# Relu sums of the sixth up product put first for all four row tiles, low parts of that quarter on GpSimd

## The chip, the cores and the metric

The kernel runs on one core of one Trainium2 chip. The metric is the device time of one execution in microseconds (us). Engines are named as in the profile: PE is the matrix engine (PEld its weight loads), DVE is VectorE, ACT is ScalarE, POOL is GpSimd, SP issues most DMAs. Each works through its own instructions in the order in which they are written; between engines an instruction waits for semaphores.

## The reference, cut to what matters

The program is a linear attention followed by two mixture layers. The change lies in the first of them, whose eight experts all run on all 2304 tokens:

```python
for e in range(E):                      # E = 8
    h = np.maximum(x @ w1[e], 0.0)      # x: 2304 x 512, w1[e]: 512 x 1024
    ye = h @ w2[e]                      # w2[e]: 1024 x 512
    out += P[:, e:e + 1] * ye
```

## The kernel before

The 2304 tokens are worked on in three blocks of 768 and each block by eight experts, so the loop over s runs 24 times; one pass is a step. Steps 8 to 22 are "fast" steps: both their products are done in seven half-size block products instead of eight (a Winograd form of Strassen's scheme), at the price of sums and differences before and after. Every float32 operand of a product is split into a high part and a low part, and a product is three matmuls: high by high, high by low, low by high.

The up products of a step (`fill`, L968) are numbered n = 0 to 6. Each has four row tiles i, and each tile is six matmuls of 384 columns into one PSUM bank. Products 1, 4 and 6 add to the banks of products 0, 3 and 5. Product 6 is the one that the change calls the sixth. Behind each tile, DVE and ACT turn the bank into the hidden layer's quarters, `hq["11"]`, `hq["12"]`, `hq["22"]` and `hq["21"]`, each with a high part [0] and a low part [1].

For tile i of product 6, with p the tile's bank, DVE adds `qs` to p in place (L1279), adds relu(p) to the buffer `s2b`, called d (L1280), writes relu(p) + u3 into `qs`, called q (L1283), and writes relu(p) - r11 into `r11`, called r (L1284). ACT rounds d into the high part `hq["21"][0]` (L1282). `run_pend()` (L1281) lets DVE do one difference left over from product 5 (L1273), only behind tile 0. Behind the last tile, DVE makes the four low parts `hq["21"][1]` from d and its high part (L1296).

Then `down` runs seven down products m = 0 to 6 of three row groups j, each 12 matmuls of 256 columns (L1104), 36 in a product. Their left operands are, in order, the quarters 11, 12, 21, and then 11, 12, 22, 21, where 11, 12 and 21 are filled anew: from `r11` by ACT at L1149 and by DVE at L1150, from `qs` by ACT at L1152 and by POOL at L1154, from `r12` by ACT at L1156 and by POOL at L1158. During product m = 0, POOL subtracts d from `r12` in four pieces (L1163). Behind products 0 and 2, ACT copies the PSUM result aside (L1123); behind product 1, DVE adds to it (L1125) and to the accumulators (L1117). For products 5 and 6 of the up stage and elsewhere, POOL makes low parts: L1274 for the quarter 22, L166 for weights. Low parts of products 1 and 4 are DVE's (L953).

PSUM: all these tiles come from one ring of six banks, `psA`, handed out in order. Each fast step takes sixteen in the up stage (four each at n = 0, 2, 3 and 5) and six in the down stage: two at m = 0 (for j = 0 and j = 2), two at m = 1, two at m = 4. So counting on from the four banks of products 5 and 6, m = 0 takes the two banks that remain, m = 1 takes the banks of tiles 0 (for j = 0) and 1 (for j = 2), and m = 4 those of tiles 2 and 3. A matmul that begins a bank waits until the last reader of its earlier tile is done.

Of the kernel before, what the change touches and what calls it, by code (L numbers as in the profile page):

```python
# [13 lines left out]
ALU = mybir.AluOpType  # L14
# [26 lines left out]
def f32(ap):  # L41
    return ap.bitcast(F32)

@with_exitstack
def tile_linattn_moe_moe(ctx: ExitStack, tc: tile.TileContext, qT, k, v, g2, wg, w1a, w2a, emb, embT, tau, w1b, w2b, out):
    nc = tc.nc
# [22 lines left out]
    def ps_a():  # L69
        return get(psA, [P, 512], F32, "A", 6)  # L70
# [61 lines left out]
    r11, r12, s2b, s5 = (rawbig[:, i * 4 * HB:(i + 1) * 4 * HB].rearrange("p (k n) -> p k n", k=4) for i in range(4))  # L132
# [430 lines left out]
    u3 = up.tile([P, 4, HB], F32, name="u3")  # L563
    rb = up.tile([P, 2, D], F32, name="rb")
    xrow = qs.rearrange("p k n -> p (k n)")
    hq = {}
# [74 lines left out]
    def run_hooks(n=1):  # L641
        for _ in range(n):
            if hooks:
                hooks.pop(0)()
# [292 lines left out]
    def open_late():  # L937
        hp4 = late.enter_context(tc.tile_pool(name="h4", bufs=1, side="right", reuse_waits="tile"))
        open_h(hp4, ("12", "22"))
        accp = late.enter_context(tc.tile_pool(name="acc", bufs=1, side="right", reuse_waits="tile"))  # L940
        accs[0] = [accp.tile([P, D], F32, name=f"acc{t}") for t in range(JT)]
# [5 lines left out]
    def run_pend():  # L947
        while pend:
            pend.pop(0)()

    def low(a, i, src):
        hh, hl = hq[a]
        nc.vector.scalar_tensor_tensor(hl[:, i, :], src, 0.0, f32(hh[:, i, :]), ALU.max, ALU.subtract)  # L953

    def hidden(a, i, ps, u, dst):
        nc.vector.tensor_tensor(dst, ps, u, ALU.add)  # L956
        run_pend()
        nc.scalar.activation(hq[a][0][:, i, :], dst, AF.Relu)  # L958
        pend.append(lambda: low(a, i, dst))

    def fill(ps, g, i, n, first, last):
        wh, wl = parts[g]
        xh, xl = x_part(n, 0), x_part(n, 1)
        j = 0
        for kk in range(2):
            fs = slice(kk * 512 + i * P, kk * 512 + (i + 1) * P)
            for a, bb in ((wh, xh), (wh, xl), (wl, xh)):
                nc.tensor.matmul(  # L968
                    ps[:, 0:HB], a[:, fs], bb[:, kk, :], start=(first and j == 0), stop=(j == 5), skip_group_check=True)
                j += 1  # L970
# [3 lines left out]
    def ahead(g):  # L974
        h = g + 3
        if h < len(seq_of):
            s, n = seq_of[h]
            if s < E or h in plain_at or n >= 7 and not quick(s):
                pool = n in POOL_LOW and (s, n) != (NSTEP - 1, 9) if s < E or not quick(s) and n >= 7 else True
                prep(h, nc.gpsimd if pool else None)  # L980
            else:
                fetch(h)
            keep(h - 1)
        for h in plain_load.get(g, ()):
            load_plain(h)
        s, n = seq_of[g]
        loads = []
        if (s < E or s == NSTEP - 1) and n < 3:
            loads = [lambda q=q: load_second(s, q) for q in (W2ORDER[0:2], W2ORDER[2:3], W2ORDER[3:4])[n]]
        if s + 1 < E and n in (3, 4, 7):  # L990
            loads = [lambda w=w: load_quarter(s + 1, w) for w in {3: ("w11", "w21"), 4: ("w22",), 7: ("w12",)}[n]]
        elif s + 1 < E and n in (5, 6):
            spare(s + 1, "s1" if n == 5 else "s2")
        for f in loads:
            if after_two:
                after_two.append([2, f])
            else:
                f()
        if s == NSTEP - 1 and n > 2:
            for f in {3: [lambda: early_w1(0), lambda: early_w1(1)], 4: [lambda: early_w1(2)], 5: [lambda: early_w1(3)],  # L1000
                      6: [lambda: early_w2(0)], 7: [lambda: early_w2(1)]}.get(n, ()):
                f()
# [35 lines left out]
    def run_thooks():  # L1038
        run_after()
        if s >= 2:  # L1040
            for f in thooks.pop(tick[0], ()):
                f()
            tick[0] += 1
# [152 lines left out]
    n_hooks = len(hooks)  # L1196
    dhooks = []
    xq = []

    for s in range(NBK * E):  # L1200
        blk, e = divmod(s, E)
# [36 lines left out]
        for n in range(7):  # L1238
            g = base[s] + n
            if s == 0 and n == 4:  # L1240
                assert len(hooks) <= n_hooks - n_att
                atts.close()
                open_late()
            for i in range(4):
                if n in (0, 2, 3, 5):
                    bank[n, i] = ps_a()
                ps = bank[{1: 0, 4: 3, 6: 5}.get(n, n), i]
                fill(ps, g, i, n, n in (0, 2, 3, 5), n in (1, 4, 6))
                p = ps[:, 0:HB]
                if n == 0:  # L1250
                    nc.scalar.copy(qs[:, i, :], p)  # L1251
                elif n == 1:
                    nc.scalar.activation(hq["11"][0][:, i, :], p, AF.Relu)
                    if fast:
                        nc.scalar.activation(r11[:, i, :], p, AF.Relu)  # L1255
                    low("11", i, p)
                elif n == 2:
                    nc.vector.tensor_tensor(qs[:, i, :], p, qs[:, i, :], ALU.add)
                elif n == 3:
                    nc.vector.tensor_tensor(u3[:, i, :], p, qs[:, i, :], ALU.add)  # L1260
                elif n == 4:
                    hidden("12", i, p, qs[:, i, :], p)
                    if fast:
                        nc.scalar.activation(r12[:, i, :], p, AF.Relu)
                elif n == 5 and not fast:
                    hidden("22", i, p, u3[:, i, :], u3[:, i, :])
                elif n == 5:
                    u = u3[:, i, :]
                    nc.vector.tensor_tensor(u, p, u, ALU.add)
                    run_pend()  # L1270
                    nc.scalar.activation(u, u, AF.Relu)
                    nc.scalar.copy(hq["22"][0][:, i, :], u)
                    pend.append(lambda i=i, u=u: nc.vector.tensor_tensor(s2b[:, i, :], u, r11[:, i, :], ALU.subtract))  # L1273
                    nc.gpsimd.tensor_tensor(hq["22"][1][:, i, :], u, f32(hq["22"][0][:, i, :]), ALU.subtract)  # L1274
                elif not fast:
                    hidden("21", i, p, qs[:, i, :], p)
                else:
                    d, r, q = s2b[:, i, :], r11[:, i, :], qs[:, i, :]
                    nc.vector.tensor_tensor(p, p, q, ALU.add)  # L1279
                    nc.vector.scalar_tensor_tensor(d, p, 0.0, d, ALU.max, ALU.add)  # L1280
                    run_pend()  # L1281
                    nc.scalar.copy(hq["21"][0][:, i, :], d)  # L1282
                    nc.vector.scalar_tensor_tensor(q, p, 0.0, u3[:, i, :], ALU.max, ALU.add)  # L1283
                    nc.vector.scalar_tensor_tensor(r, p, 0.0, r, ALU.max, ALU.subtract)  # L1284
                if i == 1:
                    ahead(g)
                if n > 0 and i == 2 and squared:
                    squared.pop(0)()
                run_hooks()
                if fast and n < 4 and dhooks:  # L1290
                    dhooks.pop(0)()
                run_thooks()
        run_pend()
        if fast:
            for i in range(4):
                nc.vector.tensor_tensor(hq["21"][1][:, i, :], s2b[:, i, :], f32(hq["21"][0][:, i, :]), ALU.subtract)  # L1296
        if e == E - 1 and blk + 1 < NBK and not fast:
            xq = x_steps(*x_stage(blk + 1))
        if e == 2 and blk == 0:
# [500 lines left out]
```

## Time and profile before

| what | us |
|---|---|
| median of 3 runs (lowest, highest) | 1817.12 (1816.57, 1821.68) |
| the profiled execution | 1814.65 |
| its span from first to last instruction | 1812.9 |
| PE busy | 1782.2 |
| DVE busy | 1253.0 |
| POOL busy | 995.5 |
| ACT busy | 845.3 |

The profiled execution's own time is 1.75 us more than its span, and 2.47 us below the median of the runs. In a timeline a row is one instruction or several like ones merged: start, time from first start to last end, engine, line, operation, what is written and read, count. A row's instructions may overlap, since the engines are pipelined.

### The profile page before, as it was taken

Reading aid. Unit: us, or ns where it says so; the run is one execution under the profiler, and the core shown is the slowest. Engines: PE = TensorE matmul, PEld = TensorE weight load, DVE = VectorE, ACT = ScalarE, POOL = GpSimd, SP = SyncE. Lnnn points to the kernel's source line nnn. Section 1 sums busy time; section 2 is a strip of 40 time slices with the busy share of each in tenths; the row PEclk is TensorE's granted clock in tenths of the full one; section 3 lists DMA queues with packets and bytes.
Section 4 is the critical chain, followed back from the end, with each engine's and each line's share of the span. In section 5 each row is a group of like instructions: output and inputs, shape, how many; then the busy total and the mean of one; then the engine's idle time right before and its main releaser. Section 6 shows DMA issues by size and latency. Waiting matters only on the chain. (4 is left out here: it accounts for less than half of the span.)

```text
span 1812.9 us, 30972 instructions
## 1 busy us (share of the span) xinstructions
PE 1782.2 (98%) x11494; PEld 1689.0 (93%) x11494; DVE 1253.0 (69%) x2196; ACT 845.3 (47%) x1435; POOL 995.5 (55%) x813
## 2 busy tenths in 40 slices
PE   7999999999999999999999999999999999999997
PEld 7889889989988999999999999999999998888996
DVE  3755596566647789876556779997567763877665
ACT  3645344344434643554444553454454433556443
POOL 1422378889879555664456475655466332543222
PEclk8999999999999999999999999999999999999999
DMA  9626267779768856556465666566465653588664
GB/s 303 219 67 210 94 226 281 252 285 333 270 244 280 285 203 222 194 190 220 166 223 193 244 224 235 188 214 215 169 213 183 229 201 109 185 315 276 231 231 154
DMA packets 185568, 397.73 MB, mean 219 GB/s; under 512 B 16448, under 2 KB 86592, under 8 KB 185408
## 3 DMA queue, kind: packets, MB, share of 16 engines
q1 hardware_dynamic: 179680, 378.33, 60.1%
q0 software_dynamic: 4000, 13.11, 2.1%
q10 hardware_dynamic: 1728, 4.23, 0.7%
q8 instruction: 92, 1.51, 0.3%
q14 instruction: 68, 0.56, 0.1%
HBM read 314.61 MB, written 81.00 MB: 218 GB/s over the span
## 5 line engine op out<-in xcount | busy, mean ns | idle before, releaser
L968 PE MATMUL A<-xo,wh 128*128 128x384 f32 x2688 | 687.8, 337 | 1.9 <-ACT qs L1251 1.4
L968 PEld LDWEIGHTS A<-xo,wh 128*128 128x128 f32 x2688 | 482.5, 188 | 4.3 <-ACT qs L1251 2.1
L968 PE MATMUL A<-xo,wl 128*128 128x384 f32 x1344 | 452.1, 336 | 1.4 <-POOL wl L166 1.4
L1104 PE MATMUL A<-wh,d 128*128 128x256 f32 x2520 | 441.4, 279 | 0.8 <-POOL d L1158 0.6
L166 POOL TENSOR_TENSOR wl<-raw,wh 128x512 fp32r<-128x512 f32 x180 | 248.9, 1405 | 284.0 <-ACT wh L161 117.4
L1104 PEld LDWEIGHTS A<-wh,d 128*128 128x128 f32 x2520 | 382.7, 188 | 4.2 <-POOL d L1158 0.8
L1104 PE MATMUL A<-wl,d 128*128 128x256 f32 x1260 | 348.7, 277 | 0.0
L968 PEld LDWEIGHTS A<-xo,wl 128*128 128x128 f32 x1344 | 252.6, 188 | 2.6 <-POOL wl L166 2.6
L1317 PE MATMUL A<-wh,d 128*128 128x512 f32 x768 | 243.8, 392 | 0.0
L1104 PEld LDWEIGHTS A<-wl,d 128*128 128x128 f32 x1260 | 236.6, 188 | 0.0
L953 DVE SCALAR_TENSOR_TENSOR d<-A,d 128x384 fp32r<-128x384 f32 x228 | 126.0, 553 | 158.1 <-ACT raw L1255 87.9
L166 POOL TENSOR_TENSOR wl<-rb,wh 128x512 fp32r<-128x512 f32 x92 | 127.5, 1407 | 161.2 <-ACT wh L161 161.2
L1317 PEld LDWEIGHTS A<-wh,d 128*128 128x128 f32 x768 | 144.2, 188 | 29.8 <-issue 0.3
L958 ACT ACTIVATE d<-A 128x384 fp32r<-128x384 f32 x132 | 65.6, 498 | 197.2 <-DVE A L956 194.9
L1317 PE MATMUL A<-wl,d 128*128 128x512 f32 x384 | 149.5, 389 | 0.0
L1251 ACT COPY qs<-A 128x384 f32<-128x384 f32 x96 | 45.7, 480 | 186.3 <-PE A L968 181.8
L161 ACT CAST wh<-raw 128x1024 fp32r<-128x1024 f32 x94 | 98.4, 1047 | 12.6 <-DMA raw<-in_w1a_dram 3.6
L260 DVE TENSOR_TENSOR wl<-raw,wh 128x1024 fp32r<-128x1024 f32 x45 | 70.8, 1575 | 35.6 <-ACT wh L259 30.3
L1317 PEld LDWEIGHTS A<-wl,d 128*128 128x128 f32 x384 | 72.2, 188 | 14.0
L956 DVE TENSOR_TENSOR A<-A,qs 128x384 f32<-128x384 f32 x132 | 73.6, 560 | 16.7 <-PE A L968 16.4
L1154 POOL TENSOR_TENSOR d<-qs,d 128x384 fp32r<-128x384 f32 x60 | 55.6, 958 | 45.5 <-ACT d L1152 45.5
L1260 DVE TENSOR_TENSOR u<-A,qs 128x384 f32<-128x384 f32 x96 | 52.1, 553 | 31.4 <-PE A L968 31.2
(496 smaller groups left out, 3365.4 us busy)
## 6 DMA issues: line engine op xcount, KB each, us to landing
raw<-in_w1a_dram SPq DMA_DIRECT2D x64, 512.0 KB, 4.4
wh<-w1c SPq DMA_DIRECT2D x64, 512.0 KB, 4.6
wl<-w1c SPq DMA_DIRECT2D x64, 512.0 KB, 5.9
wh<-w2c SPq DMA_DIRECT2D x60, 512.0 KB, 5.2
wl<-w2c SPq DMA_DIRECT2D x60, 512.0 KB, 6.0
raw<-in_w2a_dram SPq DMA_DIRECT2D x51, 512.0 KB, 4.3
raw<-in_w1b_dram SPq DMA_DIRECT2D x48, 512.0 KB, 5.4
raw<-in_w2b_dram SPq DMA_DIRECT2D x48, 512.0 KB, 4.3
```

The source lines that it names most:

```text
L161: nc.scalar.copy(hi, raw)
L166: eng.tensor_tensor(lo[:, c], raw[:, c], f32(hi[:, c]), ALU.subtract)
L260: after_two.append([2, lambda: nc.vector.tensor_tensor(lo, src, f32(hi), ALU.subtract)])
L953: nc.vector.scalar_tensor_tensor(hl[:, i, :], src, 0.0, f32(hh[:, i, :]), ALU.max, ALU.subtract)
L956: nc.vector.tensor_tensor(dst, ps, u, ALU.add)
L958: nc.scalar.activation(hq[a][0][:, i, :], dst, AF.Relu)
L968: nc.tensor.matmul(ps[:, 0:HB], a[:, fs], bb[:, kk, :], start=(first and j == 0), stop=(j == 5), skip_group_check=True)
L1104: nc.tensor.matmul(o, a[:, f, ts_], bb[:, ds_], start=(m in first and j != 1 and i == 0), stop=(i == 11), skip_group_check=True)
L1154: nc.gpsimd.tensor_tensor(a12[1][:, i], qs[:, i], f32(a12[0][:, i]), ALU.subtract)
L1251: nc.scalar.copy(qs[:, i, :], p)
L1260: nc.vector.tensor_tensor(u3[:, i, :], p, qs[:, i, :], ALU.add)
L1317: nc.tensor.matmul(ys[j], a, bb[:, ds_], start=(m + ff + i == 0), stop=(m == 3 and ff == 1 and i == 2))
```

## The change

The last two DVE operations of each tile of product 6 (q and r) are no longer issued in the tile's turn. They are kept in a list and issued behind the fourth tile, in the order q0, r0, q1, r1, q2, r2, q3, r3. The four low parts of the quarter 21 are issued to POOL instead of DVE. Nothing else is edited; the order of the matmuls and of the DMA issues stays.

```diff
                     nc.vector.scalar_tensor_tensor(d, p, 0.0, d, ALU.max, ALU.add)
                     run_pend()
                     nc.scalar.copy(hq["21"][0][:, i, :], d)
-                    nc.vector.scalar_tensor_tensor(q, p, 0.0, u3[:, i, :], ALU.max, ALU.add)
-                    nc.vector.scalar_tensor_tensor(r, p, 0.0, r, ALU.max, ALU.subtract)
+                    tails.append(lambda p=p, q=q, r=r, u=u3[:, i, :]: (
+                        nc.vector.scalar_tensor_tensor(q, p, 0.0, u, ALU.max, ALU.add),
+                        nc.vector.scalar_tensor_tensor(r, p, 0.0, r, ALU.max, ALU.subtract)))
...
         run_pend()
+        while tails:
+            tails.pop(0)()
         if fast:
             for i in range(4):
-                nc.vector.tensor_tensor(hq["21"][1][:, i, :], s2b[:, i, :], f32(hq["21"][0][:, i, :]), ALU.subtract)
+                nc.gpsimd.tensor_tensor(hq["21"][1][:, i, :], s2b[:, i, :], f32(hq["21"][0][:, i, :]), ALU.subtract)
```

## Rows read from the trace of the kernel before

**Rows 1.** Part 1 of the page: busy us, share of span, instructions.

```profile
PE 1782.2 (98%) x11494; PEld 1689.0 (93%) x11494; DVE 1253.0 (69%) x2196; ACT 845.3 (47%) x1435; POOL 995.5 (55%) x813
```

**Rows 2.** Line 1279 alone: count, ns min/median/max, first and last start.

```profile
L1279 DVE TENSOR_TENSOR A<-A,qs x60: 550/554/556, 617.5 to 1443.1; 128x384 f32<-128x384 f32 x60
```

**Rows 3.** Waits of PE from 600 to 1470: us in total, times, longest.

```profile
PE A L1104 <- POOL d L1158: 0.6, 1, 0.6
PE A L1104 <- ACT u L1123: 0.2, 1, 0.2
```

**Rows 4.** Down products 0 to 3, one step: length, busy per engine, PEclk, DMA, GB/s.

```profile
967.83:971.94 4.11, 4.11 (x37) 4.11 (x37) 4.04 (x10) 1.03 (x2) 4.11 (x5) 1.00 0.88 318
971.94:976.02 4.08, 4.08 (x38) 4.08 (x37) 4.05 (x9) 2.08 (x5) 2.05 (x3) 1.00 0.88 330
976.02:980.43 4.41, 4.41 (x39) 4.32 (x37) 4.38 (x7) 3.05 (x3) 1.87 (x2) 1.00 0.81 288
980.43:984.58 4.15, 4.15 (x39) 4.15 (x38) 0.93 (x3) 3.18 (x4) 3.98 (x5) 1.00 0.12 48
```

**Rows 5.** Timeline of PE in product 2 of that step: start, us, what.

```profile
976.59 0.39 PE L1104 MATMUL A<-wh,d 128*128 128x256 f32 x2
...
976.93 0.50 PE L1104 MATMUL A<-wh,d 128*128 128x256 f32 x2
...
977.40 0.50 PE L1104 MATMUL A<-wh,d 128*128 128x256 f32 x2
```

**Rows 6.** Timeline of DVE around the same step's up end at 967.83.

```profile
965.42 1.45 DVE L1273 TENSOR_TENSOR raw<-u,raw 128x384 f32<-128x384 f32 x1 [0.49 <-ACT u L1271]
966.79 0.55 DVE L1279 TENSOR_TENSOR A<-A,qs 128x384 f32<-128x384 f32 x1
967.38 0.56 DVE L1280 SCALAR_TENSOR_TENSOR raw<-A,raw 128x384 f32<-128x384 f32 x1
967.86 0.58 DVE L1273 TENSOR_TENSOR raw<-u,raw 128x384 f32<-128x384 f32 x1
968.36 0.55 DVE L1283 SCALAR_TENSOR_TENSOR qs<-A,u 128x384 f32<-128x384 f32 x1
968.83 0.54 DVE L1284 SCALAR_TENSOR_TENSOR raw<-A,raw 128x384 f32<-128x384 f32 x1
...
974.80 0.55 DVE L1284 SCALAR_TENSOR_TENSOR raw<-A,raw 128x384 f32<-128x384 f32 x1
975.27 2.08 DVE L1296 TENSOR_TENSOR d<-raw,d 128x384 fp32r<-128x384 f32 x4
977.27 1.75 DVE L1150 TENSOR_TENSOR d<-raw,d 128x1536 fp32r<-128x1536 f32 x1
978.93 0.69 DVE L1125 TENSOR_TENSOR A<-A,u 128x512 f32<-128x512 f32 x1
```

**Rows 7.** Timeline of ACT in the same step.

```profile
975.62 1.49 ACT L1149 CAST d<-raw 128x1536 fp32r<-128x1536 f32 x1
...
979.73 0.59 ACT L1123 COPY u<-A 128x512 f32<-128x512 f32 x1 [1.25 <-DVE A L1125]
```

**Rows 8.** Timeline of POOL in the same step.

```profile
965.16 2.87 POOL L166 TENSOR_TENSOR wl<-raw,wh 128x512 fp32r<-128x512 f32 x2
967.98 2.01 POOL L1274 TENSOR_TENSOR d<-u,d 128x384 fp32r<-128x384 f32 x2
969.95 2.00 POOL L1163 TENSOR_TENSOR raw<-raw 128x384 f32<-128x384 f32 x2
...
978.56 3.66 POOL L1154 TENSOR_TENSOR d<-qs,d 128x384 fp32r<-128x384 f32 x4 [3.03 <-ACT d L1152]
```

**Rows 9.** Down products 2 and 3 of the first fast step, as in Rows 4.

```profile
626.33:631.07 4.74, 4.74 (x38) 4.38 (x36) 4.70 (x8) 3.44 (x4) 1.82 (x2) 1.00 1.01 389
631.07:635.30 4.23, 4.23 (x38) 4.23 (x37) 4.12 (x8) 3.18 (x4) 4.05 (x5) 1.00 0.08 30
```

**Rows 10.** Timeline of DVE in that step, whose down stage starts at 618.14.

```profile
617.48 0.55 DVE L1279 TENSOR_TENSOR A<-A,qs 128x384 f32<-128x384 f32 x1
```

More of the change, by code (lines that the diff above doesn't have):

```diff
@@ L1198, in tile_linattn_moe_moe @@
     xq = []
+    tails = []
     for s in range(NBK * E):
```

## The prediction

> **What bounds the kernel now.** I read the page's busy shares first. PE works 1782.2 of 1812.9 us [rows 1], so the kernel can gain only what PE loses, and anything that makes PE wait is paid in full. The change touches the fast steps alone: line 1279 runs 60 times, four to a step, so there are 15 of them [rows 2]. Next I read PE's waits over these 15 steps: two waits, 0.8 us together [rows 3]. That looks as if nothing were to be had. But a wait that is over just before PE comes to it is not in that list, and it can still cost a little, so I cut one step, whose up stage ends at 967.83, into its down products by the clock. A product is 36 matmuls. Product 1 takes 4.08 us, product 2 takes 4.41, product 3 takes 4.15 [rows 4], for the same number and size of matmuls. I take 4.08 as the price of a product that waits for nothing.
>
> The loss in product 2 can be seen in its matmuls: a pair takes 0.39 us where nothing is late, 0.50 at 976.93 and at 977.40 [rows 5]. These are the first uses of the third and fourth low part of quarter 21. DVE makes the four low parts from 975.27 to 977.35 [rows 6], product 2 starts at 976.02, so each low part arrives within a tenth of a microsecond of its use. The matmul at 977.40 starts 0.05 after 977.35: so PE resumes 0.05 us after DVE's end, and the next matmul is 0.11 late on top (0.50 against 0.39). I use these two numbers below. Product 3 starts at 980.43, behind ACT's copy that ends at 980.32 [rows 4, 7]; that copy waits for DVE's addition to 979.62, which stands behind the long low part of `r11` (977.27 to 979.02) and so behind the four low parts [rows 6].
>
> **What the change gives.** The four low parts leave DVE and go to POOL behind L1274, which ends at 969.99 [rows 8]. Their inputs are ready early: with q and r put back, the four d follow one another. The distances of starts on DVE are 0.59 from L1279 to L1280, 0.48 from L1280 to what follows, 0.50 behind L1273, 0.47 from q to r [rows 6]. From 966.79: d0 at 967.38, the left-over difference at 967.86, then the additions at 968.36, 969.43 and 970.50 with d1 to d3 0.59 behind each, the last at 971.09. ACT rounds each in about half a microsecond, so the last high part stands near 972.2. On POOL four low parts of this form took 3.66 us elsewhere in the step [rows 8]; from 969.95 that is 973.6, while product 2 wants the first at about 976.25. They are hidden with 2 to 3 us to spare, and product 2 falls to 4.08: 0.33 gained. If ACT's copy is not late either, product 3 falls to 4.08 too: 0.07. Together 0.40 us a step.
>
> **What it costs.** The first tail on DVE, q0, now starts behind d3, at 971.09 + 0.48 = 971.57, and r0 starts at 972.04 and ends at 972.58. Before, r0 ended at 969.37 [rows 6]. r0 is the last reader of tile 0's bank, and down product 1, j = 0, is the next to begin that bank (the ring of six). PE comes to it at 971.94 [rows 4]: before, the bank had been free for 2.6 us; now it comes free 0.64 us too late. This is a new wait of PE, and all the matmuls of the step stand behind it. With 0.05 to resume and 0.11 for the matmul behind, the step loses 0.80 us. No row shows just this wait (PE held by a bank that DVE still reads). From below, the resuming costs nothing: 0.64. From above, it costs twice the 0.16: 0.96. I take 0.75, nearer to the row at 977.40, which is the same pair of engines, and a little under it because its matmul was held by an operand. The second bank, tile 1's, is free with r1 at 973.5 and is wanted two thirds into product 1: no wait. Banks 2 and 3 are wanted only by product 4.
>
> **What else is moved.** r3 ends where it did (975.35), since DVE does the same operations until there. So ACT's L1149 starts at about 975.4 instead of 975.62, and DVE's L1150 can follow at 976.9 instead of 977.27. POOL's four subtractions at L1163 move behind the low parts, from 973.6 on; at 1.0 each [rows 8] they end at 977.6. They feed ACT and POOL for quarter 21 only at product 3, and POOL's next work waits for L1152 until 978.56 [rows 8], so this delay is hidden; if L1163 ended more than a microsecond later, the low parts at L1154 would follow late. No DMA issue and no queue on SP is moved, and the transfers that start with PE's progress shift with it.
>
> **The sum.** 0.75 - 0.40 = 0.35 us lost a step. The first fast step is of the other common kind, where DVE starts product 6 later: L1279 at 617.48 [rows 10], 0.66 before the up end instead of 1.04. r0 then ends 5.79 later (972.58 - 966.79), at 623.27, and product 1 wants the bank at 618.14 + 4.11 = 622.25: 1.02 + 0.11 = 1.13 lost; products 2 and 3 took 4.74 and 4.23 [rows 9] and give back 0.66 + 0.15 = 0.81. Net 0.32: a later DVE costs at one end what it returns at the other, so I take 0.35 for every step but one. In one step PE waits 0.6 us for POOL in product 6 [rows 3]; there the new delay is swallowed. 14 x 0.35 = 4.9 us. Bounds: 0.64 - 0.40 = 0.24 and 0.96 - 0.40 = 0.56 a step, so 3.4 to 7.8. On the profiled execution, 1814.65 + 4.9 = 1819.6; on the median, 2.47 higher, 1822.0.
>
> **Rivals.** The first ends slower by more than can be told from no change (about 0.3%, 5.4 us). Two engines get in each other's way in SBUF. A DVE difference whose inputs are both in SBUF, L1273, took 1.45 us at 965.42 while POOL worked on weights, and 0.58 at 967.86 [rows 6, 8]. In its new place L1150, whose inputs are both in SBUF, asks at 976.9 while POOL's last L1163 runs until 977.6; before, POOL was idle then. If it waits for that one, it ends at 979.35 instead of 978.7, L1125 at 980.0 and ACT's copy at 980.7, just before PE now needs it (976.02 + 0.75 + 4.08 = 980.85). So the point of decision is POOL's pace: each tenth by which its eight operations end later than 977.6 is a tenth for PE in each step, with 0.11 for a resumed matmul. Were POOL half a microsecond later, the copy would end at 981.2: 0.35 + 0.05 + 0.11 more, up to 7 us in all. In the middle, 0.3 a step, it is 4.2 us more: 1826. For it speaks the 1.45; against it that one low part on POOL may take 0.8 instead of 0.92 and that the pages of the profile call POOL's spans rough.
>
> The Trainium skill, "SBUF — State Buffer", section "Who interferes with whom", speaks against the change here: it says that a DVE instruction with two SBUF inputs contends with a GpSimd instruction that reads SBUF, and the later one stands still until the first is finished. By that rule the wait of L1150 is certain, and how long it lasts is again POOL's pace; the 1.45 against 0.58 agrees with it.
>
> The second rival is faster. If product 1 did not begin tile 0's bank (a miscounted ring), or if r0 ended before 971.9 because DVE began product 6 some 0.7 us earlier, the gain would stand alone: 15 x 0.40 to 0.81, some 6 to 9 us, 1817.12 - 7 = 1810. Against it: the four banks of product 5 and the two of product 0 make the six, and DVE's start is set by the L1273 that POOL holds up, which the change leaves.
>
> **How the numbers follow.** The forecast, 1822.0, has 0.62; POOL's pace deciding, 1826, has 0.27; the gain alone, 1810, has 0.11. Of the forecast a fifth lies beyond 5.4 us, of the first rival nearly all, of the second rival a fifth lies within 0.3%. So slower 0.13 + 0.25 = 0.38, same 0.49 + 0.02 + 0.02 = 0.53, faster 0.09. The range reaches from 1818 (the lower bound with some of the runs' spread) to 1827, and leaves out the gain alone and the worst of POOL's pace.
>
> **What would show it.** Right: down product 1 begins 0.6 to 1.1 us after 36 matmuls of product 0 have gone by, behind L1284's first instance in the step; product 2 takes 4.08 with no pair at 0.50; POOL has eight operations in a row from L1274 on. The rival shows as an L1150 of more than 1.75 us and a product 3 that starts behind ACT's copy. Wrong: a down product 1 that starts on time, or a product 2 still above 4.3.

## The result, and the profile after

The changed kernel takes 1827.09 us (median of 7 runs, 1824.55 to 1833.31); the kernel before took 1816.57 beside it. The ratio is 1.0055, with a 95% interval from 1.0042 to 1.0068: slower by 10.5 us. The forecast was slower by 4.9 us, 1822.0. So the sign was right and the size was half; 1827.09 lies at the very end of the range, which reaches to 1827.

Part 1 of the page after, against [rows 1]. DVE has lost the 60 low parts (32 us busy) and POOL has gained them. PE, with the same 11494 matmuls, is busy 5 us longer, in a span that is 18.6 us longer; the profiled execution, 1833.31 us, was the slowest of the seven, while that of the kernel before, 1814.65, was 1.9 below its median.

```profile
PE 1787.6 (98%) x11494; PEld 1695.3 (93%) x11494; DVE 1220.7 (67%) x2136; ACT 850.9 (46%) x1435; POOL 1034.8 (56%) x873
```

The waits of PE from 600 to 1490, against [rows 3] (us in total, times, longest). The first line is new: PE waits for r of tile 0 (now line 1286) once in each of the 15 fast steps. The second is a weight's load that came late in one up stage.

```profile
PE A L1104 <- DVE raw L1286: 11.6, 15, 1.5
PE A L968 <- DMA wl<-w1c: 0.7, 1, 0.7
```

Two fast steps cut into down products 0 to 3, against [rows 4]. The columns are the length, the busy time of PE, PEld, DVE, ACT and POOL with counts, the granted clock, the DMA share and GB/s.

```profile
798.04:802.91 4.87, 4.28 (x37) 4.11 (x37) 4.76 (x11) 2.06 (x4) 4.87 (x7) 1.00 0.89 309
802.91:807.30 4.39, 4.39 (x36) 4.39 (x37) 2.84 (x7) 2.34 (x3) 4.39 (x5) 1.00 0.84 310
807.30:811.62 4.32, 4.32 (x38) 4.32 (x37) 3.98 (x6) 2.07 (x2) 2.74 (x5) 1.00 0.76 266
811.62:815.94 4.32, 4.32 (x38) 4.32 (x37) 0.00 (x0) 3.28 (x4) 3.33 (x4) 1.00 0.04 11
858.03:862.90 4.87, 4.27 (x38) 4.11 (x37) 4.77 (x11) 2.06 (x4) 4.87 (x7) 1.00 0.92 324
862.90:867.09 4.19, 4.19 (x37) 4.19 (x38) 2.65 (x7) 2.34 (x3) 4.19 (x5) 1.00 0.89 322
867.09:871.17 4.08, 4.08 (x39) 4.08 (x38) 4.01 (x6) 2.07 (x2) 2.71 (x4) 1.00 0.74 256
871.17:875.25 4.08, 4.08 (x39) 4.08 (x38) 0.20 (x1) 3.26 (x4) 3.44 (x4) 1.00 0.08 29
```

Product 0 has grown from 4.11 to 4.87: PE stands 0.76 us at its end. Behind it the two steps part. In the second, products 2 and 3 take 4.08, as forecast. In the first, every product behind the wait takes 4.32, with no wait in it, PE busy from end to end and a granted clock of 1.00. The timeline of PE shows why. In the first step:

```profile
802.91 0.36 PE L1104 MATMUL A<-wh,d 128*128 128x256 f32 x1 [0.59 <-DVE raw L1286]
...
805.02 0.40 PE L1104 MATMUL A<-wh,d 128*128 128x256 f32 x2
805.26 0.28 PE L1104 MATMUL A<-wl,d 128*128 128x256 f32 x1
805.38 0.40 PE L1104 MATMUL A<-wh,d 128*128 128x256 f32 x2
```

and as far behind the wait of the second:

```profile
862.90 0.36 PE L1104 MATMUL A<-wh,d 128*128 128x256 f32 x1 [0.60 <-DVE raw L1286]
...
864.93 0.39 PE L1104 MATMUL A<-wh,d 128*128 128x256 f32 x2
865.16 0.28 PE L1104 MATMUL A<-wl,d 128*128 128x256 f32 x1
865.27 0.39 PE L1104 MATMUL A<-wh,d 128*128 128x256 f32 x2
```

Three matmuls take 0.36 us in the first and 0.34 in the second. From start to start over 28 of them it is 120.0 ns in the one and 113.3 in the other; a third value, 116.7, is found in other steps (4.20 us a product). I call this the rhythm of PE. It holds from the wait to the next up stage.

DVE and POOL in the first of these steps, against [rows 6] and [rows 8]:

```profile
801.28 0.56 DVE L1281 SCALAR_TENSOR_TENSOR raw<-A,raw 128x384 f32<-128x384 f32 x1
801.75 0.55 DVE L1285 SCALAR_TENSOR_TENSOR qs<-A,u 128x384 f32<-128x384 f32 x1
802.22 0.55 DVE L1286 SCALAR_TENSOR_TENSOR raw<-A,raw 128x384 f32<-128x384 f32 x1
...
807.09 1.88 DVE L1150 TENSOR_TENSOR d<-raw,d 128x1536 fp32r<-128x1536 f32 x1 [1.55 <-ACT d L1149]
808.90 0.69 DVE L1125 TENSOR_TENSOR A<-A,u 128x512 f32<-128x512 f32 x1
```

```profile
798.18 2.01 POOL L1275 TENSOR_TENSOR d<-u,d 128x384 fp32r<-128x384 f32 x2
800.14 3.32 POOL L1300 TENSOR_TENSOR d<-raw,d 128x384 fp32r<-128x384 f32 x4
803.42 3.94 POOL L1163 TENSOR_TENSOR raw<-raw 128x384 f32<-128x384 f32 x4
```

r0 ends at 802.22 + 0.55 = 802.77, 4.73 behind the up end at 798.04, and PE starts product 1 at 802.91. The eight POOL operations run in a row and end at 807.36; L1150 asks just before that and takes 1.88 instead of 1.75.

Now the sum of each down product over the first 12 fast steps (the last three hold other work too), from the starts of the matmuls in the two traces:

| product | before, us | changed, us | difference |
|---|---|---|---|
| 0 | 49.35 | 60.21 | +10.86 |
| 1 | 48.96 | 51.63 | +2.67 |
| 2 | 54.16 | 50.64 | -3.52 |
| 3 | 50.57 | 50.64 | +0.07 |
| 4 to 6 | 148.05 | 151.91 | +3.86 |
| together | 351.10 | 365.03 | +13.93 |

At 4.08 a product, 12 of them are 48.96. Nine of the 12 changed steps run at 4.20 or 4.32 behind the wait (four and five of them), and one step of before does, from product 3 on. In the changed kernel products 2 to 6 are each 1.68 above 48.96, and product 1 is 1.71 above it besides the late matmul behind the wait (12 x 0.08 = 0.96). That is 6 x 1.68 = 10.1 us of rhythm. Without it the 12 steps would be 13.93 - 10.1 = 3.8 us slower, 0.32 a step on the average.

### The profile page after: what moved, and what is told of

Read it like the earlier page. It is cut to its first block, busy times and chain, and to the rows that moved or that the text cites. A ratio compares the mean times of both kernels' runs of the same rounds, so it can differ in the third digit from the quotient of the medians.

```text
span 1831.5 us, 30917 instructions
## 1 busy us (share of the span) xinstructions
PE 1787.6 (98%) x11494; PEld 1695.3 (93%) x11494; DVE 1220.7 (67%) x2136; ACT 850.9 (46%) x1435; POOL 1034.8 (56%) x873
## 5 line engine op out<-in xcount | busy, mean ns | idle before, releaser
L1104 PE MATMUL A<-wh,d 128*128 128x256 f32 x2520 | 448.1, 280 | 11.6 <-DVE raw L1286 11.6
L161 ACT CAST wh<-rb 128x1024 fp32r<-128x1024 f32 x46 | 48.5, 1054 | 45.7 <-PE A L1104 26.3
```

The source lines that it names most:

```text
L161: nc.scalar.copy(hi, raw)
L1104: nc.tensor.matmul(o, a[:, f, ts_], bb[:, ds_], start=(m in first and j != 1 and i == 0), stop=(i == 11), skip_group_check=True)
```

## The experiments

Theory: the loss of the change is PE's wait for tile 0's bank at product 1, and the slow rhythm that follows it; the low parts on POOL only give. Rivals: the work moved to POOL takes SBUF from others and slows PE; deferring q and r hurts in another way. All ratios are to the kernel before on the same chip. The last column is read from the one profiled execution of each run, so it need not follow the medians; in e7 and e8 it holds the added matmul.

| run | median us | ratio (95% interval) | 12 fast down stages, us |
|---|---|---|---|
| before | 1816.57 | 1 | 351.10 |
| changed | 1827.09 | 1.0055 (1.0042 to 1.0068) | 365.03 |
| e1: low parts on POOL alone | 1826.60 | 1.0054 (1.0041 to 1.0068) | 362.09 |
| e2: q and r behind alone | 1829.73 | 1.0068 (1.0049 to 1.0086) | 361.64 |
| e3: tile 0 in its turn | 1810.60 | 0.9966 (0.9953 to 0.9979) | 348.93 |
| e4: r before q | 1863.63 | 1.0253 (1.0237 to 1.0269) | 387.13 |
| e5: e3, long low part later | 1808.97 | 0.9950 (0.9937 to 0.9964) | 345.36 |
| e6: tile 0 behind tile 2 | 1811.14 | 0.9966 (0.9956 to 0.9976) | 349.08 |
| e7: changed, small matmul | 1827.03 | 1.0049 (1.0034 to 1.0065) | 361.92 |
| e8: before, small matmul | 1816.71 | 1.0000 (0.9990 to 1.0009) | 353.70 |
| e9: changed, another bank | 1814.97 | 0.9995 (0.9986 to 1.0004) | 348.87 |

**e1, one half of the change: low parts on POOL alone** (against the kernel before).

```diff
-                nc.vector.tensor_tensor(hq["21"][1][:, i, :], s2b[:, i, :], f32(hq["21"][0][:, i, :]), ALU.subtract)
+                nc.gpsimd.tensor_tensor(hq["21"][1][:, i, :], s2b[:, i, :], f32(hq["21"][0][:, i, :]), ALU.subtract)
```

> The kernel before with one edit: the four low parts of quarter 21 go to POOL, q and r stay in each tile's turn. First theory (the loss of the change is PE's wait for tile 0's bank, and whatever rhythm PE falls into behind it): r0 ends 2.6 us before down product 1 wants the bank, so product 0 keeps 4.11 us and product 1 keeps 4.08, and product 2 falls from 4.36 to 4.08. But POOL's low parts now end only at about 8.05 us behind the up end, the four differences for r12 run until about 12.0, and DVE's long low part (L1150), which asks at 9.3, has to share SBUF with them: it ends near 11.6 instead of 11.2, ACT's copy near 12.9 instead of 12.5, and product 3 waits 0.6 to 0.7 us. Net about +0.3 us a step, +5 us in all (1820 to 1824), with the lost time at product 3, none at product 1. Rival (the work moved to POOL is itself what slows the changed kernel, by taking SBUF from other engines): the same slowing as in the changed kernel, +8 to +10 us, with matmuls of more than 114 ns all through the down stage and also where nothing has waited.

Measured: 1826.60, above the expected 1820 to 1824 and in the range that the rival was given. The rows have to decide. Down products 0 to 4 of one step (columns as above):

```profile
854.82:858.93 4.11, 4.11 (x37) 4.11 (x37) 4.04 (x10) 1.03 (x2) 3.83 (x5) 1.00 0.86 290
858.93:863.01 4.08, 4.08 (x38) 4.08 (x37) 3.37 (x7) 2.08 (x5) 1.84 (x3) 1.00 0.93 327
863.01:867.83 4.82, 4.25 (x38) 4.05 (x36) 3.67 (x4) 3.04 (x3) 4.82 (x4) 1.00 0.81 276
867.83:872.14 4.31, 4.31 (x37) 4.31 (x37) 0.99 (x3) 3.18 (x4) 4.31 (x6) 1.00 0.08 30
872.14:876.34 4.20, 4.20 (x39) 4.20 (x37) 1.13 (x2) 1.32 (x2) 4.20 (x5) 1.00 0.24 60
```

and what line 1150 took in all 15 fast steps (count, ns min/median/max), and the largest of PE's waits:

```profile
L1150 DVE TENSOR_TENSOR d<-raw,d x15: 2339/2351/2355, 628.4 to 1459.5; 128x1536 fp32r<-128x1536 f32 x15
```

```profile
PE A L1104 <- ACT u L1123: 10.6, 16, 1.0
```

Products 0 and 1 are untouched; PE waits at the end of product 2, for ACT's copy, which waits for DVE, which stood in L1150 beside POOL's subtractions: 2.35 us instead of 1.75. So here the collision of the first rival is real and dear, in the place where the low parts come late. Behind that wait eight of 12 steps fall into the slow rhythm, which the expectation left out; a ninth does behind a later wait for POOL (its step has three further waits, 1.7 us together). With a matmul time of 113 ns in product 1, beside POOL at work, "POOL slows PE everywhere" falls.

**e2, the other half: q and r behind the fourth tile alone** (against the changed kernel, as all that follow unless said).

```diff
-                nc.gpsimd.tensor_tensor(hq["21"][1][:, i, :], s2b[:, i, :], f32(hq["21"][0][:, i, :]), ALU.subtract)
+                nc.vector.tensor_tensor(hq["21"][1][:, i, :], s2b[:, i, :], f32(hq["21"][0][:, i, :]), ALU.subtract)
```

> The changed kernel with one part undone: the low parts of quarter 21 are back on DVE, q and r still stand behind the fourth tile. First theory: PE waits 0.76 us (where DVE starts early) to 1.1 us for tile 0's bank as in the changed kernel, and the matmuls behind it run at 113 to 120 ns; since product 2 now starts 0.8 us later, DVE's low parts (end at 9.5 us behind the up end) are in time and product 2 shows no late pair. So about the time of the changed kernel, 1823 to 1829. Rival (the work on POOL slows the kernel): without it the loss goes, 1814 to 1818.

Measured: 1829.73, just above the expected 1823 to 1829, with the same wait of PE in the same 15 places:

```profile
PE A L1104 <- DVE raw L1286: 11.7, 15, 1.5
```

No low part on POOL is needed for the loss or for the slow rhythm (5 of 12 steps in the profiled execution). The gain at product 2 came too: it then takes 4.08 in the steps of the fast rhythm, since it starts later.

**e3, tile 0's q and r in their turn.**

```diff
                         nc.vector.scalar_tensor_tensor(r, p, 0.0, r, ALU.max, ALU.subtract)))
+                    if i == 0:
+                        tails.pop(0)()
```

> The changed kernel, but q and r of tile 0 are issued in their turn again, and only those of tiles 1 to 3 behind the fourth tile. r0 ends 1.5 us behind the up end, r1 at about 5.7 where its bank is wanted at 6.83. First theory: no wait at product 1, product 0 at 4.11 and product 1 at 4.08, and the rhythm stays at 113 ns there. Product 2 at 4.08. At product 3, DVE's long low part and the last difference on POOL ask for SBUF within 0.05 us of each other: product 3 starts on time or up to 0.75 us late. So between 1810 and 1820, below the changed kernel by 6 to 15 us. Rival (POOL): no better than the changed kernel, 1823 or more.

Measured: 1810.60, 16 us below the changed kernel, at the lower end of what was expected: product 0 is 4.11 and product 1 is 4.08 in all steps. Three of 12 steps fall into a slow rhythm at product 3, behind a matmul that comes only 0.02 us late and is in no list of waits.

**e4, another order behind the fourth tile.**

```diff
-                    tails.append(lambda p=p, q=q, r=r, u=u3[:, i, :]: (
-                        nc.vector.scalar_tensor_tensor(q, p, 0.0, u, ALU.max, ALU.add),
-                        nc.vector.scalar_tensor_tensor(r, p, 0.0, r, ALU.max, ALU.subtract)))
+                    tails.append(lambda p=p, r=r: nc.vector.scalar_tensor_tensor(r, p, 0.0, r, ALU.max, ALU.subtract))
+                    qtails.append(
+                        lambda p=p, q=q, u=u3[:, i, :]: nc.vector.scalar_tensor_tensor(q, p, 0.0, u, ALU.max, ALU.add))
...
         while tails:
             tails.pop(0)()
+        while qtails:
+            qtails.pop(0)()
```

> The changed kernel with the eight operations behind the fourth tile in another order: r0, r1, r2, r3, then q0 to q3. r0 ends 0.47 us earlier, so a dose of the suspected wait is taken away and nothing else. First theory: product 0 is 0.47 us shorter in every step (4.40 instead of 4.87 where DVE starts early), 15 x 0.47 = 7 us less than the changed kernel if the rhythm is as likely to be slow behind a short wait as behind a long one: 1818 to 1822; if a short wait leaves the rhythm alone, 1813 to 1816. Rival (POOL): no change from the changed kernel.

Measured: 1863.63, the opposite. The expectation overlooked that q0 reads the same bank: with r0 first, q0 becomes the bank's last reader, fifth in the row instead of second, 3 x 0.47 = 1.4 us later. So the run gave more of the wait instead of less: product 0 takes 6.26 instead of 4.87, as 1.4 us more would have it. Two rows of this run, products 0 and 1 of the second fast step, show something else, too:

```profile
676.84:683.25 6.41, 4.28 (x37) 4.11 (x37) 6.31 (x14) 2.06 (x4) 6.41 (x8) 1.00 0.94 337
683.25:689.05 5.80, 5.80 (x37) 5.80 (x37) 4.32 (x7) 2.23 (x3) 3.03 (x4) 0.71 0.46 176
```

PE stood idle 2.1 us, and in the product behind it the granted clock is 0.71, between its two levels of 1.2 and 2.4 GHz; the product takes 5.80 us. In seven of the first 12 steps product 1 takes 5.75 to 5.84, each at a mean granted clock of 0.70 or 0.71; in the other five, where PE stood as long, it keeps 1.00. In the changed kernel, where PE stands 0.76 to 1.64 us, it never takes more than 4.39.

**e5, the best of these: e3, and the long low part behind the first `after(1, 0)`** (against e3).

```diff
                     if m == 1:
                         nc.scalar.copy(a11[0], r11)
-                        ve.tensor_tensor(a11[1], r11, f32(a11[0]), ALU.subtract)
...
+                if m == 1 and j == 1:
+                    ve.tensor_tensor(a11[1], r11, f32(a11[0]), ALU.subtract)
```

> The run with tile 0 in its turn, and DVE's long low part (L1150) issued behind its first addition of product 1 (L1125) instead of in front of it. First theory: the addition then runs at about 7.5 us behind the up end, ACT's copy of product 2 has nothing late to wait for, and product 3 starts on time. With no wait left at products 1 to 3, products 0 to 6 all stand at 4.11 or 4.08 and the rhythm is 113 ns throughout, but for the extra work of the last three fast steps. Against the run with tile 0 in its turn that is 0.05 to 0.3 us a step and the slow rhythms of its products 3 to 6: 1803 to 1808. If the waits had nothing to do with the rhythm, products at 4.20 and 4.32 would stay and it would be 1808 to 1811.

Measured: 1808.97, 0.5% below the kernel before. That is a little above the expected 1803 to 1808 and within the 1808 to 1811 of the other answer (waits and rhythm have nothing to do with each other), so the time doesn't decide and the rows must. Products 0 to 3 of one step:

```profile
791.49:795.60 4.11, 4.11 (x37) 4.11 (x37) 4.04 (x9) 1.45 (x3) 3.83 (x5) 1.00 0.89 303
795.60:799.68 4.08, 4.08 (x38) 4.08 (x37) 4.01 (x10) 2.12 (x5) 3.70 (x5) 1.00 0.92 337
799.68:803.76 4.08, 4.08 (x38) 4.08 (x37) 3.43 (x5) 2.80 (x3) 4.08 (x3) 1.00 0.87 313
803.76:807.84 4.08, 4.08 (x38) 4.08 (x37) 0.00 (x0) 3.26 (x4) 4.08 (x6) 1.00 0.11 39
```

In 11 of the first 12 fast steps all seven products stand at 4.11 or 4.08. The other, the eighth, is the one where PE waits for POOL's low parts, in products 4 and 6. So in these 12 steps no slow rhythm is seen where nothing waits. The 13th step shows that a wait isn't needed, though. There nothing waits either, but two matmuls of 12 columns from other work stand in the row of product 2. In front of them the matmuls start 113.3 ns apart, behind them 116.7, and so to the end of the step (product 3 below them):

```profile
1323.63 0.18 PE L886 MATMUL M<-ohs,before 128*128 128x12 bf16 x1
1323.67 0.17 PE L887 MATMUL M<-incs,ones 128*128 128x12 bf16 x1
```

```profile
1326.58:1330.78 4.20, 4.20 (x39) 4.20 (x37) 2.59 (x6) 3.28 (x4) 4.20 (x5) 1.00 0.15 60
```

So what the rhythm follows is a break in the row of like matmuls, and a wait is one kind of break. The same happens in the 13th step of e3, e6 and e8.

**e6, a dose less: tile 0's q and r behind tile 2.**

```diff
+                    if i == 2:
+                        tails.pop(0)()
```

> The changed kernel, but q and r of tile 0 are issued behind tile 2 instead of behind tile 3: one DVE pair (1.06 us) earlier, so a dose of the wait is taken away. r0 then ends 4.70 us behind the first addition of tile 0 instead of 5.76: 3.66 us behind the up end where DVE starts early, 4.0 where it starts late, against 4.11 when product 1 wants the bank. First theory: the wait falls from 0.76 to 1.1 us to nothing (but for one step of the last three, 0.4), and the slow rhythm behind it goes too: 1808 to 1813. If the wait counted only by its length, the gain over the changed kernel would be 15 x 0.85 us less the 0.2 that returns, 12 us: 1814 or so. If deferring q and r mattered for another reason, it would stay near the changed kernel, above 1820.

Measured: 1811.14, as expected: r0 comes in time in 8 of 12 steps, and the loss is gone rather than 1.06 us smaller. In the other four it is 0.04 to 0.07 us late, and in two of these that is enough for the slow rhythm (products 0 and 1 of one of them):

```profile
1084.20:1088.38 4.18, 4.18 (x37) 4.10 (x37) 4.11 (x9) 2.08 (x6) 4.18 (x6) 1.00 0.94 292
1088.38:1092.78 4.40, 4.40 (x38) 4.40 (x37) 3.67 (x8) 2.13 (x6) 3.66 (x5) 1.00 1.03 417
```

**e7 and e8, what holds the rhythm.** One small matmul more in every fast step, its result not read, in front of product 2 of the changed kernel (e7) and of product 1 of the kernel before (e8).

```diff
+            if m == 2:                                # e8: m == 1
+                odd_ps = ps_m()
+                nc.tensor.matmul(odd_ps[:, 0:P], ident, ident, start=True, stop=True)
             for j in range(3):
                 product(m, j)
```

> The changed kernel with one small extra matmul (128 columns of float32, into an unused bank, its result not read) in front of product 2 of every fast step; it costs about 0.1 to 0.3 us a step. It asks what holds the slow rhythm. If the rhythm is drawn anew at any break in the row of like matmuls, products 3 to 6 change from step to step but are as mixed as before, 4.08 to 4.32, and the time is 1828 to 1832. If a break without a wait brings PE back to 113 ns, products 3 to 6 all stand at 4.08, and the time is 1818 to 1823. If something outside PE's own row sets it (traffic of POOL or DMAs), products 3 to 6 stay as slow as product 1 of the same step.

> The kernel before with the same small extra matmul in front of product 1 of every fast step, where nothing is late. If any break draws the rhythm anew, products 1 and 2 show 4.20 or 4.32 in some steps, and the time is 3 to 6 us above the kernel before; if only a wait does, products 1 stand at 4.08 to 4.2 with the cost of the one matmul, and the time is 2 to 4 us above.

e7 took 1827.03, the time of the changed kernel, between the times of the first two answers. In product 1, in front of the break, seven of the first 12 steps are slow: five at 116.7 ns and two at 120.0. Behind it products 3 to 6 stand at 4.08 in eight and at 4.20 in four (but for one product 6), never at 4.32. So the break does change the rhythm, but it doesn't bring 113 ns back each time, and it costs some 0.27 us a step itself. e8 took 1816.71, no more than the kernel before and less than either answer (2 to 4 and 3 to 6 us above): half a dozen matmuls behind the break are 1 to 9 ns slow, then it is 113 again. This break without a wait left no slow rhythm in products 1 and 2, unlike the two small matmuls of the 13th step. But in e8 seven of 12 steps run at 4.20 from product 3 on, behind the same short wait for ACT's copy that [rows 7] show, against one of 12 before. What decides between the three values stays open.

**e9, the change as it is, but another bank for product 1.**

```diff
-                ys.setdefault(k, []).append(ps_a())
+                other = m == 1 and j == 0 and s < 2 * E + 4
+                ys.setdefault(k, []).append(ps_m() if other else ps_a())
```

> The changed kernel with its order of work untouched, but in the first 12 of the 15 fast steps down product 1 begins in a free PSUM bank of the other pool instead of tile 0's bank. First theory (that bank is the cause): in these 12 steps product 0 falls from 4.87 to 5.26 us to 4.11 and products 1 and 2 stand at 4.08, with q and r as late as in the changed kernel; in the last three the wait stays (0.76, 1.5 and 0.76 us) with its slow rhythm. That is 12 x 0.85 us and the slow rhythm of these steps, 11 to 17 us below the changed kernel: 1811 to 1816. If deferring q and r hurt by another way (DVE's order, ACT's copies, SBUF), it would stay above 1822.

Measured: 1814.97, 12 us below the changed kernel (11 by the ratios), with q and r as late as there. Products 0 to 2 of one step:

```profile
789.32:793.43 4.11, 4.11 (x37) 4.11 (x37) 4.01 (x9) 1.82 (x4) 4.11 (x6) 1.00 0.85 302
793.43:797.51 4.08, 4.08 (x38) 4.08 (x37) 3.41 (x8) 1.74 (x4) 4.08 (x5) 1.00 0.86 311
797.51:801.65 4.14, 4.14 (x38) 4.05 (x36) 3.23 (x4) 2.81 (x3) 3.01 (x4) 1.00 0.78 267
```

The wait is left in the three last fast steps alone, where the old bank is kept (2.7 us, 3 times, by the waits of PE). So the bank is the cause of the wait and of the rhythm behind it. What else the order of q and r costs is small: products 2 and 3 together take 1.4 us more in the 12 steps than in e3 (102.13 against 100.76). They stand at 4.1 to 4.5 and at 4.2 to 4.3, because ACT's copy is late (1.0 us of waits, 4 times); it follows the long low part of `r11`, here line 1151, which stands beside POOL's last subtraction:

```profile
798.38 1.91 DVE L1151 TENSOR_TENSOR d<-raw,d 128x1536 fp32r<-128x1536 f32 x1 [1.55 <-ACT d L1150]
```

## Why the prediction was right, and where it was wrong

**The wait.** Right in place and cause, a little short in size. r0 ends 4.73 behind the up end in the step shown, worked out as 4.75. What was too small is the time until PE resumes. The forecast took 0.05 from the row at 977.40 and then went below the sum, to 0.75, because that row is a wait for an operand. In all 15 fast steps PE starts product 1 0.15 us behind r0's end (802.91 against 802.77 in the step shown, 0.147 before rounding). With product 0 longer by 0.76 and product 1 by 0.11 (4.19 in the steps whose rhythm stays fast) the loss is 0.87. In the first fast step 1.13 was worked out with the matmul behind; product 0 alone is 5.24 - 4.11 = 1.13 longer. The second rival, the gain alone, falls: the ring was counted rightly. e3 and e6 show that its gain is there once r0 is in time.

**The gain.** Right. Product 2 is 4.08 where the rhythm is 113 ns, and so is product 3. POOL's low parts took 0.86 each, not 0.92, and were done 3.8 us before product 2 began (803.46 against 807.30).

**The sum without rhythm.** It came out, but by luck in part. In the three of the first 12 steps whose rhythm stays fast (3, 5 and 11) the loss is 0.44 to 0.46 instead of 0.35. And the step in which PE waited for POOL, put at nothing, would give 0.8 back at that rhythm (29.46, as in step 5, against 30.27), since its wait in product 6 and its own slow rhythm are gone. The two errors nearly cancel: 11 x 0.35 = 3.85 was forecast for the 12 steps, and 3.8 was found.

**What failed** is the term behind it: that a matmul which waits for nothing takes its 4.08 us a product whatever was before it. In the profiled execution this adds 10.1 us in 12 steps to the 3.8. The two profiled executions lie 18.7 us apart, the medians 10.5, so at the median the rhythm is worth some 5 to 6 (an estimate, 10.5 less 4.9; the other executions have no trace). That the time still came to the edge of the range is no merit of the sum: the room above 1822 was left for POOL's pace, and the rhythm filled it. By the prediction's own line, 5.4 us, the result is slower, to which it gave 0.38, and not the same, to which it gave 0.53. It could have seen the rhythm: in the one step of before with such a rhythm, products 4 and 5 take 4.20 with no wait in them, behind the short wait for ACT's copy.

```profile
1042.79:1046.99 4.20, 4.20 (x38) 4.20 (x37) 4.03 (x3) 1.52 (x3) 4.20 (x4) 1.00 0.00 0
1046.99:1051.19 4.20, 4.20 (x38) 4.20 (x37) 3.30 (x7) 1.57 (x2) 4.20 (x4) 1.00 0.35 122
```

Why a break in the row leaves one of three spacings isn't known from these runs.

**The first rival** named the time that came, 1826, for a reason that didn't come. POOL's eight operations end 9.32 behind the up end, sooner than the 9.77 worked out, L1150 takes 0.14 to 0.16 us longer, and product 3 starts without a wait.

```profile
L1150 DVE TENSOR_TENSOR d<-raw,d x15: 1884/1899/1906, 628.8 to 1464.1; 128x1536 fp32r<-128x1536 f32 x15
```

The mechanism is there, hidden by the wait for the bank: in e9, without that wait, the same 1.91 makes product 3 late, and in e1, where POOL is later, L1150 takes 2.35. In all 15 fast steps of each of the three runs L1150 ends 1.61 to 1.62 us behind the end of the subtraction that POOL was at when L1150 started, whether that was 0.27 or 0.74 us away. POOL stands too: in the step of e1 shown, its subtraction that starts during L1150 takes 2.52 instead of 1.02 and ends 0.87 behind L1150. The Trainium skill, "SBUF — State Buffer", section "Who interferes with whom", says that the later of a DVE instruction with two SBUF inputs and a GpSimd one that reads SBUF stands until the other is done. These times agree with it.

**What the profile was to show**: a late product 1 behind the first r, no pair at 0.50 in product 2, eight POOL operations in a row. All three are there. A sign of being wrong is there too, a product 2 above 4.3: it takes 4.32 in five of the first 12 steps, by the rhythm and not by a late low part.

## What to carry to other kernels

Work that is put off "behind" may hold a buffer: for each deferred reader, count round the ring of banks to who begins that bank next, and when. On an engine that is busy all the time, price a wait, or any other break in a row of like work, not by its length alone, but also by the pace of the engine behind it until the next change of work. And when two halves of a change each lose, look for the one reader that decides: here tile 0's q and r in their turn, and the long low part behind the addition, make 1809 of 1827.

## What the runs showed of the hardware that was not expected

- A row of like matmuls (256 columns, weights changed for each) ran at 113.3, 116.7 or 120.0 ns from start to start, all at a granted clock of 1.00. The slow values began at a break in the row: a wait of PE, even one of 0.06 us (e6), a matmul 0.02 us late (e3), or two matmuls of 12 columns between (e5). They held until another break or the up stage with its 384 columns, 26 us in the first step shown. Some breaks left 113.3 ns (e8), and some brought it back (e7). What decides it is open.
- PE resumed 0.15 us behind the end of the DVE operation that held its bank (r0, all 15 fast steps of the changed kernel), but 0.05 us behind ACT's copy (e1, product 3, all 15).
- A DVE operation on 1536 columns with both inputs in SBUF ended 1.61 to 1.62 us behind the POOL subtraction that was under way when it started, in 45 of 45 cases (changed, e1, e9); in the kernel before it takes 1.75.
- In e4, where PE stood 2.1 us and more at the end of product 0, the next product ran at a mean granted clock of 0.70 or 0.71 in seven of the first 12 steps and at 1.00 in the other five.
